# One PSUM buffer moved to another pool, and the first instructions given a fixed order, in an attention-and-MLP kernel

## The chip, the core and the metric

The kernel runs on one core of a Trainium2 chip. The metric is the device time of one execution in microseconds (us), the median of a few runs. The core has five engines with instruction queues of their own: TensorE (PE; its weight loads are listed as PEld), VectorE (DVE), ScalarE (ACT), GpSimd (POOL) and SyncE (SP, which here only issues transfers). The program holds one list of instructions for each engine.

## The reference

```python
# attention with decay, B=8, H=8, S=576, D=64
scores = q @ k.T / sqrt(D) + (cum[:, None] - cum[None, :])   # cum = cumsum(log(clip(f, 1e-4, 1)))
scores = where(causal, -1e9, scores)
attn = softmax(scores)                   # row maximum subtracted; 1e-9 added to the row sum
x = (attn @ v)  -> [B*S, H*D] = [4608, 512]
# MLP, d_ff = 2048
h = x @ w_in
g = h * clip(h + 3, 0, 6) / 6
out = g @ w_out                          # [4608, 512], float32
```

`w_in` and `w_out` come as 64-bit floats; the rest is 32-bit. The large products are made from 16-bit pairs (a high and a low part of each operand), three matmuls for each product.

## The kernel before, in words

**Attention.** The 64 heads are worked off in the order of the list `VH`: entries 0 to 3 are "A" entries, each a pair of heads of batch 0 with its first 256 query rows; entries 4 to 11 are "B" entries, the rest of the query rows of batch 0, head by head; the other 56 are "F" entries, whole heads of batches 1 to 7. An entry v passes these stations:

- `load_x(v)` brings q and k to a buffer ST, `load_c(v)` brings two rows of cumulated decay to rows 64 and 65 of TK (for the first two pairs from the tile `cs`, later from a copy in DRAM). Both are issued on SP.
- `parts(v)` (L449, L450, POOL) rounds k and q into TK and TQ; `rests(v)` (L461 to L469: a transfer, an ACT copy, four POOL subtractions) makes their remainders.
- for A and B: `natural(v)` (L495 on PE, L501 on DVE) makes approximate scores and the maximum of each row; `max_rows(v)` transposes the maxima (L510, PE) into a tile `ptm`, DVE negates them into `mr` (L512), and a transfer (L513) brings them to row 96 of TQ; `scores(v)` (L559 to L578) makes the transposed scores with the maxima subtracted, and ACT the exponentials. For F: `rows(v)` (L619, L622 on PE, L630 to L670 on DVE, ACT and POOL).
- `av` (L702 to L713) multiplies by v and divides by the row sums; `x_move` transposes the result into xT.

**MLP.** `h_unit` makes one tile of 128 hidden columns by 12 matmuls (L788 to L790), with an epilogue on ACT and DVE (L794 to L799) into gT. `out_unit` accumulates one output tile `po` over 48 matmuls (L835 to L837), which read gT and the split w_out (`w2`), block by block. For batch 0 the first 256 rows come first: 16 h units, then two out units.

**Weights.** `w_load` (L238, SP) brings a chunk of 64-bit weights, `w_decode` (L251 to L257, ACT and DVE) makes 32-bit numbers of it and sums their squares into `wsum`; `w_sum` (L279) adds the sums, `pow2_scale` turns them into a power of two: a matmul with a matrix of ones (L184) into a PSUM tile `pt`, then four small DVE instructions (L187 to L196). `w_split` then makes the 16-bit pairs: for w_out an ACT instruction (L284) and a DVE instruction (L295) for each of 16 chunks. A chunk's pair is written over the place where the chunk before it stood as 32-bit numbers, so the 16 splits go one after the other.

**PSUM pools.** `ps_m` (tag "mm") has two buffers: for the h units' and out units' tiles and for the `pt` of the weights' scales. `ps_t` (tag "tr") has one: for `ptm`, for the `pt` of v's scales from batch 1 on, and for every third tile of later MLP units. `ps_s` has two for scores.

**What sets the order.** The text of the program gives every instruction a place; a scheduler then simulates the engines and gives each engine, whenever it is free, the ready instruction that stands first in the text. A tile gets its PSUM buffer in the same way. The order so found is fixed; on the chip each engine follows it. `tc.issue_after(ins)` adds the rule that the instructions of its block on the engine of `ins` stand behind `ins`. `small` is a list of issued small transfers; `pinned()` puts what it covers behind the last of them (the loads of v, and the first eight of w_in). The main loop calls the stations entry by entry; between them `fill` pulls h and out units, and `w_step` pulls steps of the weights' work. When the first out unit is begun (in the text this is in entry 9, behind all 16 h units and ahead of `max_rows(10)`), all of w_out's remaining work is written down at once:

```python
def moe_out(b, c0=0, c1=TT):
    if b == 0:
        for _ in wq:
            pass
```

The constants of the buffers (`init_qk(i)`, five POOL memsets each, L118 to L122; the tails of T1, L915; a part of v's buffer, L925) have nothing to wait for.

Of the kernel before, what the change touches and what calls it, by code (L numbers as in the profile page):

```python
# [11 lines left out]
F32 = mybir.dt.float32  # L12
# [3 lines left out]
ALU = mybir.AluOpType  # L16
# [4 lines left out]
def kernel(  # L21
# [10 lines left out]
    nc = tc.nc  # L32

    NHEAD, D, S = qk.shape
    D //= 2
    B = vS.shape[0]
# [3 lines left out]
    P = 128  # L40
# [15 lines left out]
    ps_m = ctx.enter_context(tc.tile_pool(name="ps_m", bufs=2, space=bass.MemoryType.PSUM))  # L56
# [6 lines left out]
    identr = cpool.tile([P, P], F32R, name="identr")  # L63
# [53 lines left out]
    def init_qk(i, eng):  # L117
        eng.memset(TQ[i].bitcast(F32)[64:96, :], 0.0)  # L118
        eng.memset(TQ[i].bitcast(F32)[64:66, :], 1.0)
        eng.memset(TK[i].bitcast(F32)[64:96, :], -1.0)  # L120
        eng.memset(TK[i].bitcast(F32)[96:97, :], 1.0)
        eng.memset(TK[i].bitcast(F32)[:, S:], 0.0)  # L122
# [25 lines left out]
    def v_chunk(b, c):  # L148
        return v_parts(b)[c // 3][:, c % 3]
# [9 lines left out]
    def decay():  # L159
        warm = p2.tile([1, 1], F32, tag="m1", name="warm")  # L160
        nc.vector.memset(warm, 1.0)
        nc.scalar.activation(warm, warm, AF.Ln)
        fs = p2.tile([NHEAD, S], F32, tag="Pp", name="fs")
        nc.sync.dma_start(fs, f)
        yield
        zf = p2.tile([NHEAD, S], F32, tag="PHL", name="zf")
        nc.vector.memset(zf, 0.0)
        nc.vector.tensor_scalar(fs, fs, 1e-4, 1.0, op0=ALU.max, op1=ALU.min)
        lf = p2.tile([NHEAD, S], F32, tag="Pp", name="lf")
        nc.scalar.activation(lf, fs, AF.Ln)  # L170
        nc.scalar.activation(warm, lf[0:1, 0:1], AF.Exp)
        cum = p2.tile([NHEAD, S], F32, tag="xf", name="cum", bufs=1)
        nc.vector.tensor_tensor_scan(cum[:, :], lf, zf, 0.0, op0=ALU.add, op1=ALU.add)
        nc.vector.tensor_scalar(cs[:, 0, :], cum, -8.0, None, op0=ALU.mult)
        nc.vector.scalar_tensor_tensor(
            cs[:, 1, :], cum, -8.0, cs[:, 0, :].bitcast(F32), op0=ALU.mult, op1=ALU.subtract
        )
        yield


    def pow2_scale(pm, s_col, i_col, name):
        pool, tag = (ps_t, "tr") if SV < s_col < SV + B else (ps_m, "mm")
        pt = pool.tile([P, 512], F32, tag=tag, name=f"pt_{name}")
        nc.tensor.matmul(pt[:, 0:1], ones, pm, start=True, stop=True)  # L184
        yield
        e = p2.tile([P, 2], F32, tag="ee", name=f"e_{name}")
        nc.vector.tensor_scalar(e[:, 0:1], pt[:, 0:1], 2.0 ** -100, None, op0=ALU.max)  # L187
        ei = e.bitcast(I32)
        nc.vector.tensor_scalar(
            ei[:, 1:2], ei[:, 0:1], 24, 23, op0=ALU.logical_shift_right, op1=ALU.logical_shift_left  # L190
        )
        si = SC.bitcast(I32)
        nc.vector.tensor_scalar(
            si[:, s_col:s_col + 1], ei[:, 1:2], -1.0, float(204 << 23), op0=ALU.mult, op1=ALU.add
        )
        nc.vector.tensor_scalar(  # L196
            si[:, i_col:i_col + 1], ei[:, 1:2], 1.0, float(50 << 23), op0=ALU.mult, op1=ALU.add
        )
        yield
# [42 lines left out]
    def w_decode(i, k, slots):  # L242

        slot = slots[k % len(slots)]
        f32 = w_chunk(i, k)[1]
        if wide:
            i32 = f32.bitcast(I32)
            hf = slot.bitcast(F32).rearrange("p (n t) -> p n t", t=2)[:, :, 1]
            lo = slot.rearrange("p (n t) -> p n t", t=2)[:, :, 0]

            nc.scalar.activation(f32, hf, AF.Prelu, scale=2.0 ** -112, alpha=2.0 ** 32)  # L251
            nc.vector.tensor_scalar(i32, i32, 3, None, op0=ALU.logical_shift_left)
            nc.vector.scalar_tensor_tensor(
                i32, lo, 29, i32, op0=ALU.logical_shift_right, op1=ALU.bitwise_or
            )
        if i == 1 or not GRAM[k // NCC]:
            nc.scalar.activation(  # L257
                slot.bitcast(F32)[:, :CW], f32, AF.Square,
                accum_out=wsum[:, NW * i + k:NW * i + k + 1],
            )  # L260
# [155 lines left out]
    def load_c(v):  # L416
        kind, n = VH[v]
        t = TK[v % NQK].bitcast(F32)[D:D + 2]
        if kind != "A":
            nc.sync.dma_start(t[:, 0:S], scr[n])  # L420
            if kind == "F":
                nc.sync.dma_start(TQ[v % NQK].bitcast(F32)[D + 2:D + 4, 0:S], scr[n])
        elif n >= 2:
            nc.sync.dma_start(
                t[:, 0:2 * QA].rearrange("r (h s) -> r h s", h=2),
                scr[2 * n:2 * n + 2, :, 0:QA].rearrange("h r s -> r h s"),
            )
        else:
            for h in range(2):
                d = nc.sync.dma_start(  # L430
                    t[:, h * QA:(h + 1) * QA], cs.bitcast(F32)[2 * n + h:2 * n + h + 1, :, 0:QA]
                )
            if PIN0:
                small.append(d.ins)
# [9 lines left out]
    def parts(v):  # L444
        i = v % NQK
        s = ST[v % NST]
        nq, nk, q0 = spans(v)
        one = dict(scalar1=1.0, scalar2=0.0, op0=ALU.mult, op1=ALU.add)
        nc.gpsimd.tensor_scalar(TK[i][0:D, 0:nk], s[D:, 0:nk], **one)  # L449
        nc.gpsimd.tensor_scalar(TQ[i][0:D, 0:nq], s[0:D, q0:q0 + nq], **one)  # L450

    def thirds(n):

# [3 lines left out]
    def rests(v):  # L457
        i, j = v % NQK, v % NL
        s = ST[v % NST]
        nq, nk, q0 = spans(v)  # L460
        nc.sync.dma_start(T7[j].bitcast(F32)[0:D, 0:nq], TQ[i].bitcast(F32)[0:D, 0:nq])  # L461
        nc.scalar.copy(T1[j][D:, 0:nk], s[D:, 0:nk])  # L462
        for a, e in thirds(nq):
            nc.gpsimd.tensor_tensor(  # L464
                T7[j][D:, a:e], s[0:D, q0 + a:q0 + e], TQ[i][0:D, a:e].bitcast(F32),
                op=ALU.subtract,
            )
        for a, e in thirds(nk):
            nc.gpsimd.tensor_tensor(  # L469
                T1[j][0:D, a:e], s[D:, a:e], T1[j][D:, a:e].bitcast(F32), op=ALU.subtract  # L470
            )
# [13 lines left out]
    def natural(v, half):  # L485
        i = v % NQK
        mc = MC[v % 2]
        grp = chunks(v)[half]
        if not grp:
            return  # L490
        pn = ps_s.tile([P, 1024], F32, tag="S", name=f"pn_{v}_{half}")
        for _, (q0, k0, r, kw, o) in grp:
            cut = [0] + [x for x in (512 - o, ) if 0 < x < kw] + [kw]
            for a, e in zip(cut, cut[1:]):
                nc.tensor.matmul(  # L495
                    pn[:r, o + a:o + e], TQ[i][0:D + 2, q0:q0 + r],
                    TK[i][0:D + 2, k0 + a:k0 + e], start=True, stop=True,
                )
        for c, (q0, k0, r, kw, o) in grp:
            junk = p2.tile([P, S], BF16, tag="junk", name=f"junk_{v}_{c}", bufs=1)  # L500
            nc.vector.tensor_tensor_reduce(  # L501
                junk[:r, :kw], pn[:r, o:o + kw], W[:r, 4 * P + r - kw:4 * P + r],
                1.0, -3.0e38, ALU.add, ALU.max, accum_out=mc[:r, c:c + 1],
            )

    def max_rows(v):
        i = v % NQK
        m = sum(len(x) for x in chunks(v))
        pt = ps_t.tile([P, 512], F32, tag="tr", name=f"ptm_{v}")
        nc.tensor.matmul(pt[:m, :P], MC[v % 2][:, 0:m], identr, start=True, stop=True)  # L510
        mr = p2.tile([NCH, P], F32R, tag="mr", name=f"mr_{v}", bufs=1)
        nc.vector.tensor_scalar(mr[:m], pt[:m, :P], -1.0, None, op0=ALU.mult)  # L512
        d = nc.sync.dma_start(TQ[i].bitcast(F32)[96:97, 0:m * P], mr.bitcast(F32)[:m])  # L513
        small.append(d.ins)

# [384 lines left out]
        next(w_in_q)  # L902
    init_qk(0, nc.gpsimd if INIT_POOL[0] else nc.vector)
    next(dec)
    load_c(0)
    parts(0)
    for i in range(2):
        nc.vector.memset(MC[i].bitcast(F32), 0.0)
        nc.vector.memset(MF[i], 0.0)
    natural(0, 0)  # L910
    init_qk(1, nc.gpsimd if INIT_POOL[1] else nc.vector)
    load_c(1)
    parts(1)
    for i in range(NL):
        nc.gpsimd.memset(T1[i].bitcast(F32)[:, S:], 0.0)  # L915
    max_rows(0)
    rests(0)
    load_x(2)
    load_v(0)
    nc.sync.dma_start(scr, cs.bitcast(F32))  # L920
    natural(1, 0)
    if W_ORDER == 2:
        next(w_in_q)
    init_qk(2, nc.gpsimd if INIT_POOL[2] else nc.vector)
    nc.gpsimd.memset(v_chunk(0, 4)[64:], 0.0)  # L925
    nc.vector.memset(pav, 0.0)

    units = []
# [148 lines left out]
```

## Time and profile before

| | |
|---|---|
| median of 3 runs | 1061.22 us (1059.41 to 1063.06) |
| the profiled execution | 1060.59 us |
| its span, first to last instruction | 1058.5 us |
| PE busy | 1006.1 us (95%) |
| DVE busy | 714.1 us (67%) |
| ACT busy | 633.0 us (60%) |
| POOL busy | 440.0 us (42%) |
| transfers, mean | 117 GB/s |

The page of the profile gives busy times, the span in 40 slices of 26.5 us, the transfers, the chain of work that ended last and the costliest groups of instructions. The other views can be asked for any stretch of time: the timeline, the busy time of each engine in a list of windows, the waits (who waited for whom), and the instructions of one line. Times in them are microseconds from the start of the span.

### The profile page before, as it was taken

The page shows a single profiled execution, that of the slowest core. Times are in us where ns is not written, and L with a number is a line of the kernel's source. Part 1 is how long each engine was busy: PE and PEld are TensorE (multiplying, and loading weights), DVE is VectorE, ACT ScalarE, POOL GpSimd, SP SyncE. Part 2 cuts the span into 40 slices and gives each one's busy share as a digit, 9 for nine tenths or more (in the row PEclk, how much of TensorE's full clock was granted, in tenths as well). Part 3 has the DMA queues.
Part 4 walks back from the last instruction along what each step waited for, and adds up shares of the span by engine and source line. Part 5 has one row for each costly group of instructions (what it writes and reads, how often), then busy time and mean ns, then how long its engine had stood idle before and what let it go on. Part 6 is the DMA issues. An engine that isn't in the chain of part 4 may idle for free.

```text
span 1058.5 us, 21322 instructions
## 1 busy us (share of the span) xinstructions
PE 1006.1 (95%) x7650; PEld 599.4 (57%) x7650; DVE 714.1 (67%) x1887; ACT 633.0 (60%) x1257; POOL 440.0 (42%) x641
## 2 busy tenths in 40 slices
PE   2799978899999999999999999999999999999998
PEld 1567845675555755555555755555555755444553
DVE  6878799876876678865885678956886677204310
ACT  5798667766864667655764667655765567205312
POOL 9634556525444444454544455544544441000000
PEclk9989989999999999999999999999999999999999
DMA  7875346936765765566565665557565644101001
GB/s 245 271 214 180 98 103 128 209 88 133 154 108 128 129 146 112 90 136 159 109 120 109 133 154 104 107 119 162 109 109 122 118 94 67 21 1 40 1 11 41
DMA packets 253717, 123.83 MB, mean 117 GB/s; under 512 B 225860, under 2 KB 227452, under 8 KB 253612
## 3 DMA queue, kind: packets, MB, share of 16 engines
q1 hardware_dynamic: 253612, 122.47, 53.0%
q8 instruction: 60, 0.98, 0.4%
q14 instruction: 45, 0.37, 0.1%
HBM read 47.93 MB, written 9.73 MB: 54 GB/s over the span
## 4 chain that ended last, share of the span: by engine, by line
PE 80%; DVE 9%; DMA 4%; ACT 4%; issue 2%; SPq 0%; POOL 0%; ACTq 0%; DVEq 0%; POOLq 0%
PE ph L788 10%; PE po L835 10%; PE po L837 10%; PE po L836 10%; PE ph L789 10%; PE ph L790 10%; PE pn L622 3%; PE pn L619 3%; PE pav L706 1%; PE pav L707 1%; PE ph_r L811 1%; PE pav L705 1%; PE ph_r L812 1%; PE ph_r L813 1%; PE po_r L835 1%
## 5 line engine op out<-in xcount | busy, mean ns | idle before, releaser
L642 ACT ACTIVATE pp<-pp,nb 128x192 f32<-128x192 f32 x280 | 138.4, 552 | 133.9 <-DVE nb L636 116.7
L788 PE MATMUL ph<-xT,w 128*128 128x512 f16 (+1 forms) x576 | 197.0, 358 | 3.6 <-ACT o L841 2.3
L659 DVE TENSOR_TENSOR ring<-pp,ring 128x128 f16<-128x128 f32 (+2 forms) x216 | 141.4, 668 | 83.5 <-ACT ring L656 77.8
L789 PE MATMUL ph<-xT,w 128*128 128x512 f16 (+1 forms) x576 | 196.3, 357 | 0.0
L790 PE MATMUL ph<-xT,w 128*128 128x512 f16 (+1 forms) x576 | 196.0, 357 | 0.0
L836 PE MATMUL po<-w,gT 128*128 128x512 f16 x512 | 192.8, 382 | 3.2 <-DVE w L295 3.2
L464 POOL TENSOR_TENSOR T<-ST,TQ 64x288 fp32r<-64x288 f32 (+2 forms) x136 | 112.4, 828 | 200.4 <-PE pn L622 152.1
L835 PE MATMUL po<-w,gT 128*128 128x512 f16 x512 | 191.0, 383 | 4.5 <-ACT w L284 3.9
L837 PE MATMUL po<-w,gT 128*128 128x512 f16 x512 | 192.3, 382 | 0.0
L630 DVE CUSTOM_DVE_ANT_0 pp<-pn,W 128x192 f32<-128x192 f32 x280 | 123.5, 484 | 33.0 <-PE pn L622 22.9
L794 ACT ACTIVATE r<-ph,bias_r,SC 128x512 f32<-128x512 f32 (+1 forms) x144 | 103.2, 726 | 64.9 <-PE ph L790 61.6
L797 DVE SCALAR_TENSOR_TENSOR r<-r,ph 128x512 f32<-128x512 f32 (+1 forms) x144 | 89.0, 621 | 75.8 <-ACT r L794 75.3
L619 PE MATMUL pn<-TK,TQ 68*128 68x192 f32 x336 | 125.9, 388 | 5.2 <-issue 4.9
L469 POOL TENSOR_TENSOR T<-ST,T 64x288 fp32r<-64x288 f32 (+1 forms) x136 | 126.0, 945 | 11.5 <-ACT T L462 6.9
L622 PE MATMUL pn<-T,T 128*128 128x192 f32 x336 | 115.8, 370 | 0.0
L656 ACT CAST ring<-pp 128x192 f16<-128x192 f32 x280 | 114.5, 450 | 0.2
L799 DVE TENSOR_TENSOR gT<-r,gT 128x512 f16<-128x512 f32 (+1 forms) x144 | 102.7, 718 | 15.5 <-ACT gT L798 13.8
L798 ACT CAST gT<-r 128x512 f16<-128x512 f32 (+1 forms) x144 | 80.9, 567 | 33.2 <-DVE r L797 32.3
L665 POOL TENSOR_TENSOR ring<-pp,ring 128x128 f16<-128x128 f32 x96 | 56.2, 585 | 104.2 <-ACT ring L656 84.3
L837 PEld LDWEIGHTS <-gT 128*128 128x128 f16 x560 | 54.7, 98 | 69.5 <-issue 9.8
L836 PEld LDWEIGHTS <-gT 128*128 128x128 f16 x560 | 54.9, 98 | 61.6 <-issue 6.6
L790 PEld LDWEIGHTS <-w 128*128 128x128 f16 x576 | 56.4, 98 | 56.6 <-issue 6.6
(159 smaller groups left out, 2036.4 us busy)
## 6 DMA issues: line engine op xcount, KB each, us to landing
ST<-in_qk_dram SPq DMA_DIRECT2D x64, 288.0 KB
ring<-in_w_out_dram SPq DMA_DIRECT2D x16, 512.0 KB
out_dram<-o SPq DMA_DIRECT2D x32, 256.0 KB
T<-TQ SPq DMA_DIRECT2D x56, 144.0 KB
vst<-in_vS_dram SPq DMA_DIRECT2D x7, 1040.0 KB
ring<-in_w_in_dram SPq DMA_DIRECT2D x9, 512.0 KB
w<-in_w_in_dram SPq DMA_DIRECT2D x7, 512.0 KB
vst<-in_vS_dram SPq DMA_DIRECT2D x14, 130.0 KB
```

The source lines that it names most:

```text
L469: nc.gpsimd.tensor_tensor(T1[j][0:D, a:e], s[D:, a:e], T1[j][D:, a:e].bitcast(F32), op=ALU.subtract)
L619: nc.tensor.matmul(dst, TQ[i][0:D + 4, qs], TK[i][0:D + 4, a:e], start=True, stop=False)
L622: nc.tensor.matmul(dst, T7[j][:, qs], T1[j][:, a:e], start=False, stop=True)
L630: nc.vector.tensor_tensor_reduce(pp[:r, w:w + kw], pn[:r, o:o + kw], W[:r, 4 * P + r - kw:4 * P + r], 1.0, -3.0e38, ALU.add, ALU.max, accu ...
L642: nc.scalar.activation(x_, x_, AF.Exp, bias=nb[:r, e0 + x:e0 + x + 1], scale=0.125)
L659: eng.tensor_tensor(hl[:r, a:a + c * P], pp[:r, at[c] + 64:at[c] + kw], hl[:r, h0[c] + 64:h0[c] + kw], op=ALU.subtract,)
L788: nc.tensor.matmul(ph, w1[0][:, cc, fs_], xh, start=(cc == 0), stop=False)
L789: nc.tensor.matmul(ph, w1[0][:, cc, fs_], xl, start=False, stop=False)
L790: nc.tensor.matmul(ph, w1[1][:, cc, fs_], xh, start=False, stop=(cc == NCC - 1))
L835: nc.tensor.matmul(po, g[:, 0, fc, ts_], w2[:, fc, 0, :], start=(fc == 0), stop=False)
L836: nc.tensor.matmul(po, g[:, 0, fc, ts_], w2[:, fc, 1, :], start=False, stop=False)
L837: nc.tensor.matmul(po, g[:, 1, fc, ts_], w2[:, fc, 0, :], start=False, stop=(fc == NFC - 1))
```

## The change

The PSUM tile of w_out's scale (`pt_w1`) is taken from `ps_t` instead of `ps_m`. The other edits concern the start. The DVE instruction L252 of the first three chunks of w_in is put behind the last instruction of `cs` (L175). `max_rows(0)` now stands in the text right behind `natural(0)`, ahead of `load_c(1)`. On POOL, `rests(0)`, `init_qk(1)` and the tails of T1 are put behind the last instruction of `parts(0)`; `init_qk(2)` and the memset in v's buffer behind that of `parts(1)`. On PE, `natural(1)` is put behind the transpose of the first maxima. Since `load_v(0)` is pinned behind the last entry of `small`, and `load_c(1)` now comes after `max_rows(0)`, v's load stands behind the transfers of `load_c(1)` and no longer behind that of the first maxima.

```diff
@@ decay
-        nc.vector.scalar_tensor_tensor(
+        last = nc.vector.scalar_tensor_tensor(
             cs[:, 1, :], cum, -8.0, cs[:, 0, :].bitcast(F32), op0=ALU.mult, op1=ALU.subtract
         )
+        small.append(last.ins)
         yield
@@ pow2_scale
-        pool, tag = (ps_t, "tr") if SV < s_col < SV + B else (ps_m, "mm")
+        pool, tag = (ps_t, "tr") if SV < s_col < SV + B or s_col == S2 else (ps_m, "mm")
@@ w_decode
-            nc.vector.tensor_scalar(i32, i32, 3, None, op0=ALU.logical_shift_left)
+            with tc.issue_after(after_cs) if i == 0 and k < 3 else nullcontext():
+                nc.vector.tensor_scalar(i32, i32, 3, None, op0=ALU.logical_shift_left)
@@ parts (returns its last instruction), max_rows (returns its matmul)
@@ the start
     next(dec)
+    after_cs = small.pop()
     load_c(0)
-    parts(0)
+    p0 = parts(0)
     for i in range(2):
         nc.vector.memset(MC[i].bitcast(F32), 0.0)
         nc.vector.memset(MF[i], 0.0)
     natural(0, 0)
-    init_qk(1, nc.gpsimd if INIT_POOL[1] else nc.vector)
+    m0 = max_rows(0)
+    with tc.issue_after(p0):
+        rests(0)
+        init_qk(1, nc.gpsimd)
+        for i in range(NL):
+            nc.gpsimd.memset(T1[i].bitcast(F32)[:, S:], 0.0)
     load_c(1)
-    parts(1)
-    for i in range(NL):
-        nc.gpsimd.memset(T1[i].bitcast(F32)[:, S:], 0.0)
-    max_rows(0)
-    rests(0)
+    p1 = parts(1)
     load_x(2)
     load_v(0)
     nc.sync.dma_start(scr, cs.bitcast(F32))
-    natural(1, 0)
-    if W_ORDER == 2:
-        next(w_in_q)
-    init_qk(2, nc.gpsimd if INIT_POOL[2] else nc.vector)
-    nc.gpsimd.memset(v_chunk(0, 4)[64:], 0.0)
+    with tc.issue_after(m0):
+        natural(1, 0)
+    with tc.issue_after(p1):
+        init_qk(2, nc.gpsimd)
+        nc.gpsimd.memset(v_chunk(0, 4)[64:], 0.0)
     nc.vector.memset(pav, 0.0)
```

More of the change, by code (lines that the diff above doesn't have):

```diff
@@ L449, in parts @@
         nc.gpsimd.tensor_scalar(TK[i][0:D, 0:nk], s[D:, 0:nk], **one)
-        nc.gpsimd.tensor_scalar(TQ[i][0:D, 0:nq], s[0:D, q0:q0 + nq], **one)
+        return nc.gpsimd.tensor_scalar(TQ[i][0:D, 0:nq], s[0:D, q0:q0 + nq], **one).ins
     def thirds(n):
@@ L509, in max_rows @@
         pt = ps_t.tile([P, 512], F32, tag="tr", name=f"ptm_{v}")
-        nc.tensor.matmul(pt[:m, :P], MC[v % 2][:, 0:m], identr, start=True, stop=True)
+        first = nc.tensor.matmul(pt[:m, :P], MC[v % 2][:, 0:m], identr, start=True, stop=True)
         mr = p2.tile([NCH, P], F32R, tag="mr", name=f"mr_{v}", bufs=1)
@@ L514, in max_rows @@
         small.append(d.ins)
+        return first.ins
     def pieces(v):
```

## The prediction, written before the changed kernel was run

> **What bounds the kernel now.** I read the page first, then windows, waits and single lines. TensorE's rows and its clock on the page, 40 slices of 26.5 us:
>
> ```profile
> PE 1006.1 (95%) x7650; PEld 599.4 (57%) x7650; DVE 714.1 (67%) x1887; ACT 633.0 (60%) x1257; POOL 440.0 (42%) x641
> PE   2799978899999999999999999999999999999998
> DVE  6878799876876678865885678956886677204310
> PEclk9989989999999999999999999999999999999999
> ```
>
> TensorE is the bound: 1006.1 of 1058.5 us, and from slice 9 on nothing else can matter. What it lacks lies in slices 1 to 8, and there in two places: the start (slices 1 and 2) and slices 6 to 8, where DVE's digits are 9, 9 and 8 while PE falls to 7 and 8. The windows (PE, PEld, DVE, ACT, POOL busy, then granted clock, transfers) divide the second place:
>
> ```profile
> 110.00:132.00 22.00, 22.00 (x186) 19.33 (x186) 15.75 (x38) 14.66 (x28) 10.92 (x15) 1.00 0.38 106
> 140.00:147.00 7.00, 2.50 (x14) 1.21 (x13) 6.94 (x14) 6.61 (x15) 4.74 (x6) 0.95 0.24 66
> 147.00:154.00 7.00, 3.76 (x14) 2.24 (x13) 6.50 (x20) 2.24 (x6) 1.80 (x3) 0.50 0.42 80
> 132.00:198.00 66.00, 49.60 (x397) 32.11 (x396) 62.91 (x179) 45.76 (x95) 43.95 (x53) 0.89 0.62 136
> 198.00:264.00 66.00, 65.52 (x569) 45.07 (x569) 49.15 (x156) 43.72 (x96) 27.83 (x38) 0.98 0.64 129
> ```
>
> Up to 132 TensorE is full while DVE idles 22.00 - 15.75 = 6.25 us. From 132 to 198 it is the other way round: DVE idles 66 - 62.91 = 3.09 us, TensorE 66 - 49.60 = 16.4 us, and its clock is 0.89. After 198 TensorE is full again and DVE has 66 - 49.15 = 16.85 us free. So a DVE-bound stretch lies between two PE-bound ones. The waits from 132 to 198 name what TensorE lacks first:
>
> ```profile
> ACT w L284 <- DVE w L295: 9.4, 4, 5.1
> PE po L835 <- ACT w L284: 3.9, 2, 3.5
> PE po L836 <- DVE w L295: 3.2, 3, 1.7
> ```
>
> These are the splits of w_out. The first out units stand and wait for them.
>
> **The change, first part: `pt_w1` in the other pool.** Why are the splits so late? The lines of their chain, each with its count, durations (min/median/max ns) and first and last start:
>
> ```profile
> L279 DVE TENSOR_REDUCE wm<-wsum x5: 146/147/156, 28.1 to 110.8; 128x1 f32<-128x4 f32 x4, 128x1 f32<-128x16 f32 x1
> L788 PE MATMUL ph<-xT,w x64: 269/273/285, 84.2 to 128.5; 128*128 128x256 f16 x64
> 130.94 0.73 DVE L797 SCALAR_TENSOR_TENSOR r<-r,ph 128x256 f32<-128x256 f32 x2
> L184 PE MATMUL pt_w<-wm,ones x10: 196/250/352, 29.1 to 133.8; 128*128 128x1 f32 x10
> L510 PE MATMUL ptm<-identr,MC x12: 219/269/667, 16.2 to 122.0; 128*3 128x128 f32 x8, 128*4 128x128 f32 x4
> L284 ACT ACTIVATE w<-w,SC x16: 705/718/724, 139.6 to 191.1; 128x512 f16<-128x512 f32 x16
> L295 DVE SCALAR_TENSOR_TENSOR w<-w,SC x16: 734/743/1405, 141.4 to 193.9; 128x512 f16<-128x512 f32 x16
> ```
>
> The sum w_out's scale needs is ready at 110.8 + 0.15 = 110.95; its matmul with the ones starts with the last pair of records at 133.8, nearly 23 us later. In the text it stands behind the 16 h units of the first 256 rows (64 records of L788, the last at 128.5), and these hold the two "mm" buffers in turn; the last two are read out by L797 until 130.94 + 0.73 = 131.67. That TensorE was merely busy doesn't explain it: `ptm` of entry 11, later in the text, ran at 122.0 in the one-buffer pool. So I take the wait to be for an "mm" buffer, though the trace shows no wait for a buffer as such. In `ps_t` the matmul can run at about 111 to 112.
>
> What follows is a chain: 139.6 - 133.8 = 5.8 us from the matmul to the first split, then 16 times an ACT and a DVE instruction in turn, 16 x (0.718 + 0.743) = 23.4 us at least. It took 55 us (139.6 to 194.6) since DVE was full. Begun at 117 it ends at 140.4 at the earliest; I assume about 145. The out units, whose buffers come free at 131.67, then find half of their blocks split and need not wait: 3.9 + 3.2 us of waits go, and the 96 matmuls that were strewn from 140 to 195 become a dense load for TensorE while DVE catches up.
>
> The splits cost DVE 16 x 0.743 = 11.9 us wherever they run. Price of moving them: DVE's 6.25 idle us up to 132 take half of them; the other half pushes work of B entries back (maxima, row sums, and ACT's exponentials behind 11.5 us of L284). Cover for this on TensorE are the h units still to come, with their epilogue's rows from 110 to 132 and the first unit's first and last matmul:
>
> ```profile
> L799 DVE TENSOR_TENSOR gT<-r,gT 128x256 f16<-128x256 f32 x8 | 3.8, 479 | 2.1 <-ACT gT L798 1.9
> 111.09 0.28 PE L788 MATMUL ph<-xT,w 128*128 128x256 f16 x1
> 112.30 0.27 PE L790 MATMUL ph<-xT,w 128*128 128x256 f16 x1
> ```
>
> Eight units of 112.57 - 111.09 = 1.5 us remain, and the out units follow. Without that cover TensorE loses the 5.6 us that don't fit.
>
> Bounds of the gain. Upper: all of TensorE's idle time, 16.4 us, or with the clock back at 1.00 another 49.6 x 0.11 = 5.5 us. By DVE alone, doing the same work before the state that is now reached at 198: 6.25 + 3.09 = 9.3 us. Lower: none, if the buffer wasn't the wait; below nothing, see the rivals. I take **8 us**, near the DVE bound, because the row of 132 to 198 says DVE binds; 6.25 us of its idle time is really opened to the splits, and about half of the 3.09 us of waits should stay.
>
> The clock weighs on this. In the window 147 to 154, behind TensorE's longest halts, the granted clock is 0.50, against 1.00 up to 132. [...]
>
> The new pool has one buffer: `ptm` of entry 10 now waits until DVE has read `pt_w1`, with everything behind it on TensorE. DVE's reading followed 1.1 us after the matmul, with DVE full:
>
> ```profile
> 134.87 0.15 DVE L187 TENSOR_SCALAR e_w<-pt_w 128x1 f32<-128x1 f32 x1
> 112.33 0.30 PE L510 MATMUL ptm<-identr,MC 128*3 128x128 f32 x1
> ```
>
> `ptm` stood at 112.33, 1.4 us after the sum is ready, so one h unit's matmuls cover it: 0 us, 1.1 if not.
>
> **Second part: the start.** The timeline (start, duration) and POOL's constants up to 10.8 us (count, busy, mean):
>
> ```profile
> 8.17 0.77 DVE L252 TENSOR_SCALAR gT<-gT 128x512 int32<-128x512 int32 x1
> 9.68 2.70 SPq L430 DMA_DIRECT2D TK<-cs  x4
> 10.81 1.03 POOL L449 TENSOR_SCALAR TK<-ST 64x512 fp32r<-64x512 f32 x1
> 11.90 0.69 POOL L450 TENSOR_SCALAR TQ<-ST 64x512 fp32r<-64x512 f32 x1
> 12.65 1.22 PE L495 MATMUL pn<-TK,TQ 66*128 66x128 f32 x4 [12.65 <-POOL TQ L450]
> 18.18 0.68 SPq L513 DMA_DIRECT2D TQ<-mr  x1
> 21.34 0.95 POOL L450 TENSOR_SCALAR TQ<-ST 64x512 fp32r<-64x512 f32 x1
> 22.14 0.58 PE L559 MATMUL ps<-TQ,TK 97*128 97x256 f32 x1 [1.84 <-DMA TQ<-mr]
> 26.38 1.75 DVE L366 TENSOR_REDUCE vm<-v 128x1 f32<-128x1536 f32 x1 [2.00 <-DMA v<-in_vS_dram]
> L120 POOL MEMSET TK<- 32x640 f32 x3 | 2.2, 729 | 0.0
> L118 POOL MEMSET TQ<- 32x640 f32 x3 | 1.9, 645 | 0.2
> L121 POOL MEMSET TK<- 1x640 f32 x3 | 1.9, 627 | 0.2
> L925 POOL MEMSET xT<- 64x520 f32 x1 | 0.8, 802 | 0.0
> L915 POOL MEMSET T<- 128x64 f32 x2 | 0.2, 158 | 0.1
> 34.00:80.00 46.00, 40.56 (x207) 28.60 (x207) 36.51 (x123) 43.06 (x89) 23.66 (x30) 0.89 0.82 238
> ```
>
> POOL fills three sets of buffers before it rounds the first pair. Two thirds of 2.2 + 1.9 + 1.9, and 0.8 + 0.2, go behind the rounding: 5.0 us, so that TQ is ready at 12.59 - 5.0 = 7.6. Next is late what comes from `cs`: L252 (0.77) no longer stands in front of its last step, so the transfers start at 8.9 instead of 9.68. Their landing isn't shown; it lies between the issue of the second (half of the 2.70 on, at 11.0) and 12.65, hence now 10.3 to 11.9. TensorE starts 0.75 to 2.3 us earlier. The transfer of the first maxima and the scores follow, sooner by that and by what SP's queue lets go. v's load goes onto SP ahead of that transfer: three issues more in front of it, but DVE's 2.00 us halt for v goes.
>
> POOL's work is not less, only later: the second set and its rounding keep their place, and the third pair's rounding, which ended at 21.34 + 0.95 = 22.29, now has the third set ahead of it and comes no sooner, up to 0.8 us (L925) later. And from 34 to 80 ACT is full (43.06 of 46), with weights that come by SP. So between -0.8 and the 2.3 + 2.00 = 4.3 us that the start itself can win, I carry **2 us** to the end: the halt for v, the one wait that goes without POOL being asked.
>
> **Sum.** 1060.59 (the profiled execution) - 8 - 2 = 1050.6. It lay 0.6 below the median of 1061.22, so a median of **1051** is forecast. The case's own range: gains of 3 (DVE's waits alone) to 9.3 + 4.3, that is 1047 to 1058.
>
> **Rivals.**
> - *The splits only trade places.* TensorE is at 22.00 of 22.00 up to 132: perhaps `pt_w1` was late by priority, or DVE, bound all through, gives back after 132 what it took before. For it: no row names the buffer. Against: 6.25 idle us of DVE. Gain 2 us from the start: 1059.
> - *Slower: the splits crowd out attention.* They stand ahead of entries 9 to 11 in the text; ACT and DVE give them 16 x 1.46 = 23.4 us first. TensorE is left with eight h units of 1.5 us, 12 us, and halts for 11.4; it gets back only the 7.1 us of out-unit waits, and no start. 1061 + 4.3 = 1065. It decides once TensorE idles over 9 us between 111 and 136. For it: that text order. Against: a split occupies DVE only half of the time, and ACT has 7.3 us free up to 132.
> - *TensorE stays dense.* The rows of later F entries are put off past 198, where DVE has 16.85 us free; all of 16.4 + 5.5 is won, with the start's 2: 1037. Against: in the text, h units of the next 256 rows come late. [...]
>
> **How the numbers follow.** Forecast 0.60, trading places 0.18, slower 0.12, dense 0.10. I call anything within 0.3% (3.2 us) the same, about what a measurement of this kernel can tell. Faster: 0.60 less 0.03 at its weak end, plus 0.10: 0.67; same 0.18 + 0.03 = 0.21; slower 0.12. The range 1043 to 1060 leaves out the slower case and most of the dense one, 0.2.
>
> **What would show it.** Right: L184's last `pt_w` record near 112 (earlier by the start's gain), L284's first near 117, L295's last before 150; the waits of L835 and L836 for the splits gone; PE full between 140 and 180, the clock at 1.00; DVE over 0.9 from 111 on. At the start: L450's first end near 7.6, the first L495 at 10.4 to 11.9, no DVE halt before L366. Wrong: `pt_w1` still near 130; or TensorE idle between 111 and 136; or the first h units of the second 256 rows (now at 198) not earlier by more than the start's gain.

## The result and the profile after

The changed kernel takes 1049.55 us (median of 4 runs, 1048.52 to 1053.45) against 1061.26 us for the kernel before (4 runs). The ratio is 0.9887, 95% interval [0.9866, 0.9907]: 12.0 us faster, at least 9.9 (the medians differ by 11.7). The profiled execution took 1048.52 us, with a span of 1046.7. 1051 was forecast. The end is right; how the two parts of the change make it is not what was forecast, as the experiments show.

The page of the changed kernel, the lines that answer to those of before (totals, then 40 slices of 26.2 us):

```profile
PE 1002.6 (96%) x7650; PEld 596.2 (57%) x7650; DVE 711.4 (68%) x1887; ACT 632.7 (60%) x1257; POOL 448.3 (43%) x641
PE   2899997999999999999999999999999999999998
DVE  7778798998767778867875778846895677204310
PEclk9899999999999999999999999999999999999999
```

The span splits into TensorE's busy time and the rest. The rest went from 1058.5 - 1006.1 = 52.4 to 1046.7 - 1002.6 = 44.1 us: 8.3 us less idle time. The busy time fell by 3.5 us although the same 7650 matmuls run. That fits the clock: a matmul at half rate stays busy for longer (1.91 us against 1.02 for two 128x512 products), and there is less half rate (17.1 us up to 300 instead of 27.3; both below, at the table). Together 11.8 us, the whole difference of the two spans. Slices 6 to 8, which were 7, 8 and 8, now read 9, 7 and 9.

The same windows as before the change (PE, PEld, DVE, ACT, POOL busy, then clock and transfers), with 132 to 160 by itself:

```profile
110.00:132.00 22.00, 21.83 (x177) 18.05 (x175) 17.15 (x44) 15.06 (x32) 9.93 (x14) 1.00 0.39 106
132.00:160.00 28.00, 26.52 (x173) 16.42 (x171) 24.88 (x71) 19.00 (x37) 18.57 (x22) 1.00 0.36 82
132.00:198.00 66.00, 57.80 (x518) 42.12 (x516) 59.10 (x175) 51.61 (x111) 43.03 (x51) 1.00 0.64 137
198.00:264.00 66.00, 61.49 (x527) 37.46 (x526) 61.68 (x180) 48.78 (x103) 42.36 (x59) 0.97 0.86 171
```

From 132 to 198 TensorE now idles 8.2 us instead of 16.4, at a clock of 1.00 instead of 0.89. Some of it returns behind 198: 4.5 us idle where there was 0.5, with VectorE at 61.68 of 66 us (49.15 before). VectorE's load was moved, not taken away (711.4 us in all, 714.1 before).

The chain of the splits in the changed kernel, by lines (count, durations in ns, first and last start), and then the waits from 132 to 198 (total us, times, longest):

```profile
L281 DVE TENSOR_REDUCE wm<-wsum x5: 135/144/158, 17.8 to 114.2; 128x1 f32<-128x4 f32 x4, 128x1 f32<-128x16 f32 x1
L185 PE MATMUL pt_w<-wm,ones x10: 169/260/372, 18.0 to 117.0; 128*128 128x1 f32 x10
L286 ACT ACTIVATE w<-w,SC x16: 711/724/726, 119.5 to 162.6; 128x512 f16<-128x512 f32 x16
L297 DVE SCALAR_TENSOR_TENSOR w<-w,SC x16: 732/750/1356, 120.2 to 165.6; 128x512 f16<-128x512 f32 x16
```

```profile
ACT w L286 <- DVE w L297: 8.9, 6, 2.8
PE po L839 <- DVE w L297: 1.5, 3, 0.6
PE po L838 <- ACT w L286: 0.7, 1, 0.7
```

`pt_w1` leaves 2.8 us after its sum (117.0 and 114.2); before it was 23. The splits start 20 us earlier, and the out units wait for them 2.2 us instead of 7.1. But the sum came 3.4 us later than before, and the splits took 47 us, not the 23 to 28 that the prediction assumed.

The start of the changed kernel, from its timeline (start, duration, what was waited for):

```profile
5.31 0.61 POOL L452 TENSOR_SCALAR TQ<-ST 64x512 fp32r<-64x512 f32 x1
8.98 2.67 SPq L432 DMA_DIRECT2D TK<-cs  x4
13.09 1.19 PE L497 MATMUL pn<-TK,TQ 66*128 66x128 f32 x4 [13.09 <-DMA TK<-cs]
16.17 1.75 DVE L368 TENSOR_REDUCE vm<-v 128x1 f32<-128x1536 f32 x1 [0.32 <-DMA v<-in_vS_dram]
17.84 0.15 DVE L281 TENSOR_REDUCE wm<-wsum 128x1 f32<-128x4 f32 x1
18.04 0.58 PE L185 MATMUL pt_w<-wm,ones 128*128 128x1 f32 x2 [3.76 <-DVE wm L281]
```

The rounding is done at 5.9 instead of 12.6, and it gains nothing at that place: the first products start at 13.09 (12.65 before), now held by the transfers from `cs`. What did move is further down. On VectorE the sum for w_in's first scale stands right behind the maximum over v. With v here 10 us earlier, that scale leaves at 18.04 instead of 29.13, and the first h unit starts at 77.1 instead of 84.2. The prediction has no term for that.

### The profile page after: what moved, and what is told of

It is laid out like the page before. It is cut to its first block, busy times and chain, and to the rows that moved or that the text cites. A ratio compares the mean times of both kernels' runs of the same rounds, so it can differ in the third digit from the quotient of the medians.

```text
span 1046.7 us, 21331 instructions
## 1 busy us (share of the span) xinstructions
PE 1002.6 (96%) x7650; PEld 596.2 (57%) x7650; DVE 711.4 (68%) x1887; ACT 632.7 (60%) x1257; POOL 448.3 (43%) x641
## 4 chain that ended last, share of the span: by engine, by line
PE 79%; DVE 11%; ACT 4%; issue 2%; DMA 2%; POOL 2%; SPq 0%; ACTq 0%; DVEq 0%; POOLq 0%
PE ph L791 9%; PE ph L792 9%; PE ph L793 9%; PE po L838 9%; PE po L840 9%; PE po L839 9%; PE pn L625 3%; PE pn L622 3%; DVE pp L633 2%; PE ph_r L814 1%; PE ph_r L815 1%; PE ph_r L816 1%; PE pav L709 1%; PE po_r L838 1%; PE po_r L840 1%
## 5 line engine op out<-in xcount | busy, mean ns | idle before, releaser
L791 PE MATMUL ph<-xT,w 128*128 128x512 f16 (+1 forms) x576 | 198.0, 359 | 3.3 <-DVE r L800 1.6
L662 DVE TENSOR_TENSOR ring<-pp,ring 128x128 f16<-128x128 f32 (+2 forms) x216 | 136.8, 646 | 87.0 <-ACT ring L659 82.9
L471 POOL TENSOR_TENSOR T<-ST,T 64x288 fp32r<-64x288 f32 (+1 forms) x136 | 129.9, 974 | 6.7 <-ACT T L464 1.2
L625 PE MATMUL pn<-T,T 128*128 128x192 f32 x336 | 114.0, 364 | 0.0
L802 DVE TENSOR_TENSOR gT<-r,gT 128x512 f16<-128x512 f32 (+1 forms) x144 | 103.5, 721 | 13.7 <-ACT gT L801 11.9
L668 POOL TENSOR_TENSOR ring<-pp,ring 128x128 f16<-128x128 f32 x96 | 59.8, 623 | 112.1 <-ACT ring L659 93.6
L839 PEld LDWEIGHTS <-gT 128*128 128x128 f16 x560 | 54.7, 98 | 60.4 <-issue 5.5
```

The lines of the kernel that those rows point to most:

```text
L471: nc.gpsimd.tensor_tensor(T1[j][0:D, a:e], s[D:, a:e], T1[j][D:, a:e].bitcast(F32), op=ALU.subtract)
L625: nc.tensor.matmul(dst, T7[j][:, qs], T1[j][:, a:e], start=False, stop=True)
L662: eng.tensor_tensor(hl[:r, a:a + c * P], pp[:r, at[c] + 64:at[c] + kw], hl[:r, h0[c] + 64:h0[c] + kw], op=ALU.subtract,)
L791: nc.tensor.matmul(ph, w1[0][:, cc, fs_], xh, start=(cc == 0), stop=False)
L839: nc.tensor.matmul(po, g[:, 0, fc, ts_], w2[:, fc, 1, :], start=False, stop=False)
```

## Experiments

Twelve kernels were run, four at a time, each four beside 17 runs of the kernel before (medians 1061.30, 1061.12 and 1061.10 us). The theory at the outset was the prediction's: two separate gains, a large one from the pool and a small one from the start. The rivals: the start carries nearly all, or each part needs the other.

In the table, ratios are to the kernel before, with 95% intervals; the other columns are of the profiled execution: the span, TensorE's busy time, its idle time between 110 and 300 us (summed over the gaps ahead of its instructions), and the time up to 300 us that the clock's record shows at half.

| kernel | ratio | span | PE busy | idle 110-300 | half rate |
|---|---|---|---|---|---|
| before | 1 | 1058.5 | 1006.1 | 16.9 | 27.3 |
| changed | 0.9887 [0.9866, 0.9907] | 1046.7 | 1002.6 | 12.9 | 17.1 |
| 1 pool alone | 0.9934 [0.9920, 0.9948] | 1055.0 | 1006.9 | 11.5 | 30.7 |
| 2 start alone | 1.0064 [1.0048, 1.0080] | 1070.7 | 1010.3 | 25.4 | 34.1 |
| 3 changed, v late | 0.9958 [0.9938, 0.9978] | 1060.3 | 1014.0 | 11.3 | 34.1 |
| 4 before, v's maximum later | 1.0106 [1.0092, 1.0120] | 1071.4 | 1017.0 | 19.2 | 61.4 |
| 5 changed, low halves on GpSimd | 1.0114 [1.0085, 1.0143] | 1070.4 | 1008.6 | 26.4 | 37.5 |
| 6 start alone, low halves on GpSimd | 1.0194 [1.0176, 1.0212] | 1080.8 | 1011.7 | 36.5 | 41.0 |
| 7 before, scores' pool | 0.9980 [0.9965, 0.9994] | 1058.3 | 1007.9 | 15.2 | 34.1 |
| 8 changed, no pins on GpSimd | 1.0071 [1.0055, 1.0088] | 1069.7 | 1013.4 | 16.6 | 47.8 |
| 9 before, units in another order | 1.0163 [1.0143, 1.0183] | 1074.2 | 1011.9 | 20.6 | 30.7 |
| 10 start alone, units in another order | 1.0185 [1.0164, 1.0206] | 1077.3 | 1013.8 | 24.1 | 37.5 |
| 11 changed, units in another order | 1.0135 [1.0116, 1.0154] | 1070.3 | 1007.5 | 23.5 | 37.5 |
| 12 changed, second pair not pinned | 1.0024 [1.0011, 1.0037] | 1064.6 | 1008.7 | 19.2 | 44.4 |

Two things have to be read with the table. The record of the clock begins late: its first entry is full rate from 40.5 us on in before, 31.0 in the changed kernel, 39.3, 32.0, 48.3 and 22.3 in kernels 1 to 4. Ahead of it the matmuls have the durations of half rate: two 128x512 products of L287 take 1.91 us at 35.84 in before, 1.91 at 45.57 in kernel 1, where the record shows half rate, and 1.02 at 42.62 in before, where it shows full rate. So this first stretch comes on top of the last column, and it is 9.5 us shorter in the changed kernel. TensorE is busy in it for 11.9 us instead of 17.9; those 6.0 us of work take about half as long at full rate, which is some 3 us less busy time, an estimate from these durations. And span less busy time, the whole idle time, tells halts from slow matmuls. Kernel 2 loses by halts (60.4 us idle, 52.4 in before). Kernels 3 and 4 have little more idle time than the kernels they are made from (46.3 against 44.1, 54.4 against 52.4), but 11.4 and 10.9 us more busy time.

### 1 and 2: each part by itself

The pool alone, on the kernel before:

```diff
-        pool, tag = (ps_t, "tr") if SV < s_col < SV + B else (ps_m, "mm")
+        pool, tag = (ps_t, "tr") if SV < s_col < SV + B or s_col == S2 else (ps_m, "mm")
```

> The kernel before with one edit alone: w_out's scale product takes its result buffer from the pool of the maxima's transposes; nothing of the start is touched. Theory A, that of the prediction, the two parts of the change are separate gains: pt_w1 leaves at 111 to 113 instead of 133.8, the splits of w_out start about 20 us earlier, the half-clock stretch at 146 to 157 goes, and the time falls by 6 to 9 us (ratio 0.991 to 0.994). Theory B, the start carries nearly all and the splits only trade places with attention's work on VectorE: 0 to 1.5 us. Theory C, each part needs the other: under 3 us here and under 3 us for the start alone.

Measured: 7.0 us faster (5.5 to 8.5). `pt_w1` left at 118.5, the splits ran from 121.7 to 157, and no wait for a split is left. Theory A's time holds for this part. Its way there holds less well: the product came later than 111 to 113, since its sum came at 114.0 and it left 4.5 us behind that, and the half-rate stretch at 146.4 went but another of 10.24 us stands at 172.4.

The start alone is the changed kernel with that line put back.

> The changed kernel with w_out's scale product put back into the pool of the matmuls: all edits of the start, without the other pool. The first h unit comes near 77 instead of 84. Theory A (separate gains): TensorE's idle time before 34 falls by 3.6 us and that is kept, 3 to 4.5 us faster than before (0.9958 to 0.997), with pt_w1 still behind the 16 h units at 125 to 131. Theory B (the start carries nearly all): 9 to 11 us faster. Theory C (each needs the other): what the start gains is waited for again at the splits, under 1.5 us.

Measured: 6.8 us **slower** (5.1 to 8.5). No theory had that sign. Its profiled execution was the longest of its six runs (1072.55; 1065.92 to 1072.55), but even the shortest, at the highest granted clock of the six (0.992), lies above all runs of before. The first h unit came at 82.1 and not near 77, and `pt_w1` at 137.1. So the parts aren't separate. On top of the pool the start brings 5 us (0.9887 against 0.9934, whose intervals don't overlap); without it, it costs 7. On top of the start the pool brings 19 us (0.9887 against 1.0064); without it, 7. A weak form of theory C is left: the start needs the pool.

The windows of the start alone show the place of the loss, and the waits from 132 to 222 a part of the cause:

```profile
132.00:198.00 66.00, 49.68 (x409) 32.59 (x408) 60.57 (x169) 47.68 (x97) 44.16 (x53) 0.92 0.58 130
198.00:264.00 66.00, 56.92 (x492) 39.42 (x492) 53.44 (x160) 46.05 (x103) 32.33 (x47) 1.00 0.69 136
```

```profile
PE po L839 <- DVE w L297: 9.1, 5, 4.4
PE po L838 <- ACT w L286: 1.8, 1, 1.8
```

Up to 198 it idles as before (16.3 us). Then the kernel before was full, 65.52 of 66, and this one lacks 9 us. The splits start at 144.4 and end at 205, and the out units wait 10.9 us for them. That is 4 us more than before and doesn't explain 9 by itself.

### 3 and 4: what in the start counts

```diff
-        with pinned() if PIN_V else nullcontext():
+        with tc.issue_after(small[-1 if b else -2]):
```

> The changed kernel with one thing of the start undone: the transfer of the values of the first batch waits again for the transfer of the first pair's maxima, as before. Theory V: w_in's first sum stands behind the maximum over the values on VectorE, so the early landing of the values (16 instead of 26) is what brought w_in's first scale from 29 to 18 and the first h unit from 84 to 77; then here the scale is back at 26 to 29, the first h unit at 82 to 85, and 2 to 4 us of the gain are lost (ratio to before 0.991 to 0.993). Theory P (the reordered pinned instructions on GpSimd and VectorE bring it): h first stays at 77 to 79 and the ratio stays at 0.988 to 0.990.

Measured: 0.9958, so 7.5 us of the 12 are gone. From the timeline of its profiled execution (1062.09 us, the second longest of twelve):

```profile
26.64 1.75 DVE L368 TENSOR_REDUCE vm<-v 128x1 f32<-128x1536 f32 x1 [1.15 <-DMA v<-in_vS_dram]
28.51 0.13 DVE L281 TENSOR_REDUCE wm<-wsum 128x1 f32<-128x4 f32 x1
30.59 0.48 PE L185 MATMUL pt_w<-wm,ones 128*128 128x1 f32 x2
```

Theory V holds in kind: the first scale is late again, with v, and the first h unit starts at 89.7. The loss is about twice the upper end of its estimate, but much of it comes with the clock. Runs of the same granted clock lie closer together: at 0.990 kernel 3 took 1052.23 us and the changed kernel 1048.71 and 1050.39, at 0.986 kernel 3 took 1053.66 and 1055.68 and the changed kernel 1053.45. That leaves 0 to 4 us for the late v itself. Why most runs of kernel 3 got less clock isn't shown.

The next kernel brings the scale forward in another way: in the kernel before, the maximum over v is asked for one entry later.

```diff
-        next(vq, None)
+        if i: next(vq, None)
...
-        next(vq, None)
+        if i: list(vq) if i == 1 else next(vq, None)
```

> The kernel before with one edit: the maximum over the first batch's values is asked for one pair later in the text, so that on VectorE w_in's first sum stands ahead of it; no pin, no pool is changed. Theory V: the first scale leaves at 16 to 19 instead of 29, the first matmuls of w_in's low parts follow at 20 to 24 and the first h unit comes at 76 to 80; TensorE's idle time before 34 falls by 3 us or more and the kernel is 2 to 4 us faster than before. Theory P (the pinned first instructions do it): the first scale may move, but the time stays within 0.1%.

```profile
14.92 0.16 DVE L279 TENSOR_REDUCE wm<-wsum 128x1 f32<-128x4 f32 x1 [0.64 <-ACT w L257]
15.13 0.59 PE L184 MATMUL pt_w<-wm,ones 128*128 128x1 f32 x2 [1.74 <-DVE wm L279]
26.32 1.75 DVE L366 TENSOR_REDUCE vm<-v 128x1 f32<-128x1536 f32 x1 [1.61 <-DMA v<-in_vS_dram]
```

The scale leaves at 15.1, earlier than anywhere, and the kernel is 11 us slower: the later scales come at 50.6, 69.7 and 92.2 (47.9, 67.9 and 83.7 before), the first h unit at 95.1, and the record shows 61.4 us at half rate. Theory V's second half falls. An early first scale by itself is worth nothing. Of the 12.9 us that the span is longer, 10.9 are busy time, so here too it is slower matmuls more than halts. That an early scale pays where the chunks behind it and the attention keep up is a guess that no run tests.

### 5 and 6: is VectorE's load the limit?

```diff
-    POOL_REST = ((0, 0, 0, 0), (0, 0, 0, 0))
+    POOL_REST = ((0, 0, 0, 0), (0, 1, 0, 1))
```

> The changed kernel with the low halves of every second split of w_out subtracted on GpSimd instead of VectorE (8 of 16; ScalarE gets one more copy of 128x512 for each, about 0.71 us; GpSimd about 1.7 us for each). Theory D: from 110 to 222 VectorE is the bound (after: 17.15 of 22, 24.88 of 28, 34.22 of 38, 23.9 of 24 us), so 8 x 0.74 = 5.9 us less on it gives TensorE 2 to 5 us: ratio to before 0.984 to 0.987. Theory O: what counts is the order of the instructions that comes out, not the amount of VectorE's work; the splits' chain then gets longer by GpSimd's slower subtraction and the time stays within 2 us of the changed kernel's or gets worse.

> The start's edits alone (7 us slower than before, splits from 144 to 204, TensorE waits 10.9 us for them and VectorE is busy 23.2 of 24 us from 198 to 222) with the same 8 low halves on GpSimd. Theory D (VectorE is the bound of that stretch, and the late splits fall on it together with the attention's rows): 4 to 8 us faster than the start alone, ratio to before 0.999 to 1.003. Theory O (the order decides): within 2 us of the start alone, 1.0045 to 1.0085.

Measured: 12 and 21 us slower than before. Theory D, as it was put, falls: 6 us less work on VectorE in the splits made them slower as a chain. In kernel 5 they run from 122.1 to 203 instead of 119.5 to 166, in kernel 6 from 138.2 to 221; the out units wait for GpSimd now as well (2.6 and 5.4 us), whose subtraction takes 1.16 us where VectorE's instruction takes 0.75. (The 1.7 us expected agree with L471 of the changed kernel on GpSimd, 0.97 us for 64x288, scaled to 512 columns.) With the splits the idle time grew, from 12.9 to 26.4 and from 25.4 to 36.5. The edit made VectorE's load smaller and the chain of splits longer at once, so it doesn't tell what less load alone would do.

### 7 and 8: another pool, and the pins on GpSimd

```diff
-        pt = pool.tile([P, 512], F32, tag=tag, name=f"pt_{name}")
+        if s_col == S2:
+            pool, tag = ps_s, "S"
+        pt = pool.tile([P, 1024 if tag == "S" else 512], F32, tag=tag, name=f"pt_{name}")
```

> The kernel before with one edit: w_out's scale product takes its result buffer from the pool of the scores instead of that of the matmuls. Theory A' (any pool that the h units do not hold will do; the product was late for a buffer): pt_w1 leaves at 110 to 118, the splits follow, and the time falls as with the maxima's pool, 5 to 9 us (0.9915 to 0.995). Theory O (the gain is that of one lucky order): anything from 0.99 to 1.008, without the splits' start as its measure.

`pt_w1` left at 114.8, 2.2 us after its sum, and the splits ran from 117.8 to 151: this pool frees it as well, so the wait before was for a buffer. TensorE's lists say the same of all kernels: where `pt_w1` is in the "mm" pool (before and kernels 2, 4, 6, 9 and 10) it stands behind all 192 matmuls of the 16 h units, in another pool behind 9 to 13 units. (The wait is one in the scheduler's simulation; on the chip the product only follows its list.) But the gain is only 2.1 us (0.6 to 3.7): early splits aren't the whole story. The windows of this kernel show where it goes:

```profile
132.00:160.00 28.00, 28.00 (x160) 16.17 (x159) 17.65 (x48) 14.79 (x28) 9.19 (x12) 1.00 0.17 52
160.00:198.00 38.00, 28.29 (x286) 24.15 (x284) 35.81 (x102) 28.27 (x64) 26.34 (x33) 0.82 0.72 153
```

Up to 160 TensorE is full with out units, and VectorE has 10 us free; then VectorE is full, and TensorE lacks 9.7 us and falls to 0.82. That is the prediction's rival of traded places, in one kernel. The pool alone has the same pattern, more mildly.

```diff
-    with tc.issue_after(p0):
-        rests(0)
-        init_qk(1, nc.gpsimd)
-        for i in range(NL):
-            nc.gpsimd.memset(T1[i].bitcast(F32)[:, S:], 0.0)
+    rests(0)
+    init_qk(1, nc.gpsimd)
+    for i in range(NL):
+        nc.gpsimd.memset(T1[i].bitcast(F32)[:, S:], 0.0)
...
-    with tc.issue_after(p1):
-        init_qk(2, nc.gpsimd)
-        nc.gpsimd.memset(v_chunk(0, 4)[64:], 0.0)
+    init_qk(2, nc.gpsimd)
+    nc.gpsimd.memset(v_chunk(0, 4)[64:], 0.0)
```

> The changed kernel without the two pins on GpSimd (the rounding's rests, the constants of the second and third pair no longer held behind the first and second pair's rounding); the early values, the pins on VectorE and TensorE and the pool stay. Theory V (the early values and the other pool make the gain): ratio 0.988 to 0.991, first scale at 18 to 21. Theory P (the pins on GpSimd make a good part of it): the first pair's products start 2 us or more later than 13.1 and 3 us or more of the gain are lost, 0.9915 or more.

Measured: 7.5 us slower than before, 20 slower than the changed kernel. A free buffer isn't enough for an early product: `pt_w1` left at 126.7, 12.9 us after its sum (113.8), with 13 h units ahead of it in the list; why, is not shown. The pins matter more than theory P said, and elsewhere: the first products start at 13.10, as in the changed kernel. The second pair's wait 3.2 us for GpSimd, and from 34 to 110 TensorE idles 12.7 us (7.3 in the changed kernel) at a clock of 0.80 (0.91).

### 9 to 12: the order of the units

By now the reading was this. The feed-forward units are taken in order, so late splits hold the out units and with them the h units of the next 256 rows. Meanwhile only the attention's rows run, and these are VectorE's work. The other order:

```diff
+    def drain():
+        for _ in wq:
+            pass
+        yield 0.1
...
-                units.append(moe_out(0, 0, QA))
+                units.append(drain())
...
             units.append(moe_in(b, cut, TT))
+            if b == 0: units.append(moe_out(0, 0, QA))
```

> The kernel before with another order of its feed-forward units: the two out units of the first 256 rows stand behind the 16 h units of the second 256 rows instead of ahead of them; pools and start as before, pt_w1 still behind the first 16 h units. Theory Q: the units are taken in order, so late splits of w_out hold the two out units and with them all later units; until then only the attention's rows run, these are VectorE's work, and TensorE idles and falls to half its clock. Here nothing waits for the splits: h units of the second rows run from 140 to 150 on, the half-clock stretch between 140 and 200 shrinks, TensorE's idle time from 110 to 300 falls from 16.9 to 13 or less, and the time falls by 3 to 8 us (0.9925 to 0.997). Rival R: the place of the out units is only traded (without them TensorE has nothing but attention from 128 to 140): within 2 us of before, or slower.

> The start's edits alone (7 us slower than before) with the same other order of the units. Theory Q: what the start gains is lost alone because attention, some 5 us ahead, runs on longer by itself while the out units wait for the splits; with nothing waiting, the start's gain stays: as fast as the kernel before in that order or up to 5 us faster than it, ratio to before 0.988 to 0.997. Rival R (the start's order itself costs the 7 us, wherever the units stand): 5 us or more slower than the kernel before in that order.

> The changed kernel (start and pool) with the same other order of the units. Theory Q: the pool has already freed the out units (TensorE waits 2.2 us for splits), so the other order gives little here, and may cost what the out units cover from 124 to 151: ratio to before 0.986 to 0.992, and the pool's worth in this order (against the start's edits alone in it) is under 4 us where it is 19 us in the old order. Rival R: the pool keeps its 15 us or more in this order too.

Measured: all three are slower than before, by 17, 20 and 14 us. As a forecast of times theory Q falls in all three, and rival R is right that the out units are missed from 128 on. One window of kernel 11 shows it:

```profile
132.00:160.00 28.00, 14.88 (x124) 12.89 (x123) 27.30 (x74) 19.95 (x41) 20.71 (x24) 0.71 0.37 85
```

With no out units beside it, the attention fills VectorE (27.30 of 28) and leaves TensorE at 14.88 and a clock of 0.71. (11.29 us of that idle time are one halt, for which the profile names no releaser.) As to the difference between the three, Q comes near. Where nothing waits for the splits, the pool is worth 5 us on top of the start (1.0135 against 1.0185), not 19, and the start costs 2 instead of 7 (1.0185 against 1.0163, with intervals that overlap).

The last kernel takes away the pin of the second pair:

```diff
-    with tc.issue_after(m0):
-        natural(1, 0)
+    natural(1, 0)
```

> The changed kernel without the pin that holds the second pair's score products behind the first pair's maxima transposes; all else stays. Theory S (each pin decides only how early the first pairs come, so the span moves by what TensorE's idle time before 110 moves, 26.4 us in the changed kernel): within 3 us of the changed kernel, 0.986 to 0.992. Rival L (any other order of the start shuffles the order after 110, and this sets the time): 0.993 to 1.008 with the idle time before 110 within 2 us of the changed kernel's.

Measured: 2.5 us slower than before, 14.5 slower than the changed kernel. Idle time before 110 rose by 5.0 us to 31.4 and behind 110 by 6.3. Theory S falls, and L too in its second half: both stretches moved.

### What the twelve say together

The attention runs at VectorE's pace: from 160 to 200 VectorE is busy for 38.20, 36.18, 36.86 and 38.64 of 40 us in before, in the changed kernel, in the pool alone and in the start alone. The DVE instruction that reads the scores of a row piece (five pieces to a head, two records to a piece) in these 40 us, in the same order:

```profile
160.00:200.00 40.00, 8.84 (x40) 0.93 0.73 162
```

```profile
160.00:200.00 40.00, 8.93 (x40) 1.00 0.84 178
```

```profile
160.00:200.00 40.00, 9.04 (x41) 0.87 0.71 153
```

```profile
160.00:200.00 40.00, 8.84 (x40) 1.00 0.77 169
```

It is 20 pieces in 40 us, so 10 us to a head, in all four. What differs is what TensorE has beside it. In TensorE's list of instructions one can count the whole heads that stand between the 16th h unit and the third whole h unit of the next rows: 7.1 before, 8.0 in the start alone, 8.1 and 9.7 in kernels 5 and 6, but 4.0 in the changed kernel and 2.8 to 3.7 in kernels 1, 3, 7, 8 and 12, where the splits come early. Idle time from 110 to 300 goes with it: 16.9 us at 7.1 (19.2 in kernel 4, also 7.1), 25.4 at 8.0, 26.4 at 8.1, 36.5 at 9.7. That is 6 to 9 us for each head that runs ahead without units. Where the splits come early, or nothing waits for them, the count doesn't tell the idle time: it is 11.3 to 19.2 us in kernels 1, 3, 7, 8 and 12, and 20.6 to 24.1 in kernels 9 to 11, whose count is 3.0.

Among the kernels with early splits it seems to be the split of the work that decides. From 132 to 160 the pool alone makes 5 pieces and the changed kernel 10:

```profile
132.00:160.00 28.00, 2.27 (x10) 1.00 0.34 78
```

```profile
132.00:160.00 28.00, 4.39 (x20) 1.00 0.36 82
```

So the pool alone leaves more of the attention for later, the transposed rows of the next units come late, TensorE waits 4.3 us for them at 173.5, and the clock is at half from 172.4 to 182.7. In the changed kernel the out units and the attention run side by side from 124 to 165, no halt there exceeds 1 us, and the clock stays up until 249.

**Shown:** the parts depend on each other; the product waited for a buffer; a late v holds the first scale; the attention alone doesn't fill TensorE (14.88 of 28 us in kernel 11). **Argued only:** that the start gives attention a lead, which the pool lets run beside the out units, and which without the pool becomes one more head run ahead. The counts and the three differences fit it, but no run sets the lead by itself, since each edit at the start reorders all that follows and shifts the clock as well (17.1 to 61.4 us at half rate in the table). Why the scheduler lays the out units dense in kernels 1 and 7 and mixed in the changed kernel stays open. None of the twelve beats the changed kernel.

## Why the prediction was right, and where not

- **The wait was for an "mm" buffer: right.** Two other pools free the product; it leaves 2.2 to 4.5 us after its sum in kernels 1 and 7. "About 111 to 112" came out as 117.0, because the sum itself came at 114.2. That sum stands at 110.8, 110.0 and 114.0 in before and kernels 9 and 1, whose lists are alike up to there: it goes with the clock, 0.93, 0.96 and 0.89 from 34 to 110.
- **Gain of 8 from the pool: right in size.** 7.0 us by itself. The bound by VectorE's free time (9.3) wasn't passed there. The 7.1 us of waits went as forecast in kernel 1; what replaced a part of them is the wait for the transposed rows.
- **Splits over before 150: wrong.** The assumed length of 28 us was 36 in the pool alone and 47 in the changed kernel. It cost little: the out units waited for splits for 2.2 us.
- **`ptm` of entry 10 covered: right.** It ran at 118.4, and TensorE had 21.83 of 22 us up to 132.
- **The start, 2 us: the step that failed.** Its mechanism was "TensorE starts 0.75 to 2.3 us earlier" and "DVE's 2.00 us halt for v goes". TensorE started 0.44 later, as the `cs` transfers released it only at 13.09, past the forecast 11.9, with nothing gained from the rounding. The halt shrank from 2.00 to 0.32, but what counted was the instruction behind it, the first scale's sum. And the term was carried to the end as a number of its own: it is minus 7 without the pool and plus 5 with it. The sum held because 7 + 5 is near 8 + 2, and that is luck: nothing in the prediction makes the start worth more with the pool than without it.
- **Rivals.** Traded places: seen in kernel 7, and mildly in 1. Slower by crowded-out attention: TensorE idles 0.2 us from 110 to 132 and 1.5 from there to 160, not over 9, so not here. TensorE stays dense: no, it is busy for 57.80 of 66 us.
- **Signs.** The clock was at 1.00 from 140 to 180, as said, but TensorE was not full (33.98 of 40). VectorE was at 0.78, 0.90 and 0.93 in the three windows from 110, 132 and 198, not over 0.9 from 111 on. The rounding ended at 5.9, not near 7.6. The h units of the second 256 rows were misread: the first stood at 139.6 before and only the second at 198.0. Now the first is at 151.2, so later, but the second is at 168.1, and the last matmuls of the 16 came at 203.5 instead of 223.6.

## What to carry to other kernels

Where two kinds of work share the engines, one bound by VectorE and one by TensorE, ask of each edit what runs beside what afterwards, not only which wait goes: the same lead at the start was worth minus 7 or plus 5 us. Look at what stands directly behind a halted instruction on its engine, since a late load can cost more through its neighbour: the maximum over v waited for 2.00 us, the scale behind it came 11 us late. And where a scheduler fixes the order, measure each part alone before adding up terms; edits of the same kind moved this kernel by minus 12 to plus 21 us.

## What was not expected of the hardware

TensorE's longest wait in the prediction's rows is 3.5 us. In the changed kernel half rate stands behind shorter halts too. One of 2.42 us is followed by 10.24 us at half rate, although TensorE is busy in 9.46 of 10 us of it:

```profile
40.75 0.22 PE L512 MATMUL ptm<-identr,MC 128*4 128x128 f32 x1 [2.42 <-DVE MC L503]
```

```profile
41.40:51.40 10.00, 9.46 (x33) 6.97 (x33) 8.27 (x34) 8.21 (x17) 7.20 (x6) 0.50 0.84 261
```

Halts of 1.73 and 1.82 us (at 98.1 and 248.4) are followed by 3.41 us. The length of a halt doesn't decide it alone: no half rate follows the halt of 1.70 us at 182.1, nor those of 2.08 and 2.15 us in kernel 1 (at 198.2 and 228.2). In the 3.41 us ahead of the three falls TensorE was busy for 0.99, 1.68 and 1.51 us. What else decides it is not shown. The recorded stretches at half rate ahead of 300 us are 10.24, 10.24, 3.41 and 3.41 us long in before and 10.24, 3.41 and 3.41 in the changed kernel; those at the very end are 3.1 and 4.0. In every row of the table the half rate is a multiple of 3.41 us, to within 0.1: 5 times in the changed kernel, 8 in before, 18 in kernel 4.

The clock also goes with the scatter of runs. Kernels 2 and 10 have the same list for TensorE's first 721 matmuls, yet from 59.4 to 69.4 one profiled execution was at half rate and the other was not:

```profile
59.40:69.40 10.00, 10.00 (x34) 7.08 (x33) 5.67 (x23) 7.61 (x15) 4.28 (x6) 0.50 0.51 158
```

```profile
59.40:69.40 10.00, 9.71 (x64) 7.05 (x62) 7.01 (x28) 9.03 (x17) 4.55 (x6) 1.00 0.64 207
```

34 matmuls against 64 in the same 10 us, and the first h unit at 82.1 against 78.1. Over the 12 runs of kernel 3, the time goes against the mean granted clock (correlation -0.85): 1052.4 us at 0.993, 1063.9 us at 0.983. A single profile of this kernel can therefore lie several us off for a reason that is not in the program; the one of kernel 3 lies 6.5 us above the median.
